# State-space scan and maxout FFN on one core: output pieces between the seam's y products, earlier output-weight decoding, later masks and exponents for the second chunk

## The chip, the cores and the metric

The kernel runs on one core of one Trainium2 chip. The metric is the device time of one execution in microseconds, and the time of a kernel is the median of its runs. The five engines of the core are called PE (matmul; PEld is its weight load), DVE, ACT, POOL and SP (which here only issues DMAs). Each engine takes its instructions strictly in the order in which the program gives them, and waits for others through semaphores.

## The reference

```python
# batch 4, heads 8, sequence 768, head_dim 32, d_state 16
log_a = np.log(np.clip(a, 1e-06, 1.0))
for c in range(nc):
    cum = np.cumsum(la, axis=-1)
    L = np.exp(cum[:, :, :, None] - cum[:, :, None, :]) * causal
    CB = np.einsum('bhin,bhjn->bhij', Cc, Bc)
    y_intra = np.einsum('bhij,bhjd->bhid', CB * L, xc)
    y_inter = np.einsum('bhin,bhnd->bhid', Cc, state) * np.exp(cum)[..., None]
    y[:, :, sl] = y_intra + y_inter
    state = decay_full * state + np.sum(Bx, axis=2)      # Bx: B x, decayed to the chunk's end
x = y.transpose(0, 2, 1, 3).reshape(3072, 256)           # the bridge
h = np.maximum(np.maximum(x @ w1, x @ w2), x @ w3)       # 256 -> 768
out = h @ w_out                                          # 768 -> 256
```

The weights come in 64-bit floats and are turned into 32-bit ones on the chip.

## The kernel before

The sequence is cut into six chunks of 128 tokens (all four batches and eight heads at once, so a chunk is 512 rows of the FFN). A chunk passes through the scan (transposes of B and C, scores s, masked decays L, state A, output y) and then through the FFN. The order of all instructions is written out by hand; nothing reorders them. While PE works on the FFN of one chunk, the pieces of the scan of the next one are put between its matmuls.

Chunk 0 and chunk 1 differ from the rest:

- **Chunk 0's FFN** is a loop over 18 groups (`for n in range(NF * 3)`, lines 1044 to 1105). A group is four matmuls of 128x512 in the trace (L648, two of the program's, each in two passes): one weight matrix, one 128-column slice. Groups 2j and 2j+1 use the weights that step j of the decoding has produced. Into these groups the scan of chunk 1 is placed: masks, exponents, transposes (`transposed(1)` at group 11), scores (group 12), state sums (group 14).
- **The decoding of a weight block** has six instructions on three engines: ACT L184 and L193, DVE L185 and L188, POOL L194 (`decode()`), and then DVE L197 (`sign()`), which writes the 32-bit block. There are nine blocks for w1 to w3 and three for `w_out`. A block is fetched by one DMA of 512 KB (L168).
- **The decays of chunk 1.** `decay_load` (L390) brings the sums of log a into the tile L by DMA; `decay_masks(1, 0)` and `decay_masks(1, 2)` (L405, POOL, two instructions each, one pair of batches each) write the causal mask; `part(1)` (L415, ACT, four instructions each, eight parts in all) takes the exponents; `scan_weight` (L560, DVE) multiplies the scores in. `pop` takes these and other postponed DVE steps from a list.
- **The seam** (lines 1106 to 1118) is the stretch between the last group of chunk 0 and the first group of the FFN of chunk 1. There PE forms y of chunk 1: `scan_old` (L572, 32 matmuls) and `scan_own` (L588, 64 matmuls in two calls of 32). Then ACT copies y out of PSUM (`scan_y`, L615), DVE forms sums of it (`scan_sums`, L623), and these feed the first group of chunk 1. B of chunk 2 is transposed in between (`transposed(2, False)`, L434).
- **Output pieces.** `down_next()` issues one of twelve pieces of chunk 0's output (L884, two matmuls of 128x256, four in the trace). Six pieces belong to one half u of the output. Within a half, pieces one and two read the first decoded block of `w_out`, three and four the second, five and six the third. Each half collects in one PSUM bank, of which there is one (`ffn_bank`). When a half is complete ACT copies it out (L889), and only then can the next half start.
- **The FFN of chunk 1** runs over nine groups k (`early` L713 to 727, `late` L729 to 745; seven matmul products L698 in place of eight). The tables X1, Y1, P1, D1, K1 say what goes where in these groups: X1 and Y1 name the output pieces ("D") and scan steps ahead of and behind `late`, P1 how many postponed steps are popped at three places, D1 which exponents (L415) of chunks 2 and 3 are taken, K1 the masks.

Sum banks, exponents and copies: in each group ACT first copies a sum out of PSUM (L723, in `early`), then takes D1's exponents, and then comes whatever X1 gives it.

Of the kernel before, what the change touches and what calls it, by code (L numbers as in the profile page):

```python
# [19 lines left out]
def kernel(  # L20
# [25 lines left out]
    NB, NH, S, D = x.shape  # L46
# [42 lines left out]
    def att_bank(shape, name):  # L89
        turn["att"] += 1  # L90
        if shared["att"] and turn["att"] % 5 == 0:
            return bank("sumA", 1, shape, name)
        return bank("att", 4, shape, name)
# [112 lines left out]
    def decode():  # L206

        first, second = decode_steps()
        first()
        unsigned.append(second)  # L210

    def sign():

        unsigned.pop(0)()
# [186 lines left out]
    def decay_masks(c, b0):  # L401

        b = slice(b0, b0 + 2)
        for rows, base in ((P, HP), (HP, 0)):
            nc.gpsimd.affine_select(  # L405
                out=Ls[c][0:rows, b], in_=Ls[c][0:rows, b],
                pattern=[[0, 2], [0, NH], [1, HP]], compare_op=ALU.is_ge, fill=MASKED,
                base=base, channel_multiplier=-1)
# [153 lines left out]
    def scan_old(c):  # L562


        st = blocks[c]
        st["y"] = ys = [[att_bank([P, NB, HP], "y") for _ in range(2)] for _ in range(KD)]
        for b in range(NB):
            for u, S in enumerate((states[c], middle[c])):
                for r in range(NP):
                    rows = slice(r * PN, (r + 1) * PN)  # L570
                    q = r % 2 * 2 * D
                    nc.tensor.matmul(  # L572
                        out=ys[r // 2][u][q:q + 2 * D, b],
                        lhsT=S[rows, b].rearrange("p g d -> p (g d)"),
                        rhs=st["Cd"][rows, b, u * HP:(u + 1) * HP],
                        start=(b == 0), stop=False, tile_position=(r * PN, q),
                        skip_group_check=True)

    def scan_own(c, bs=range(NB)):

        st = blocks[c]
        M = Ls[c]
        for b in bs:
            for h in range(NH):
                t, q = divmod(h, QH)
                for u in range(2):
                    rows = slice(u * HP, (u + 1) * HP)
                    nc.tensor.matmul(  # L588
                        out=st["y"][t][u][q * D:(q + 1) * D, b],
                        lhsT=st["x"][rows, b * NH + h], rhs=M[rows, b, h],  # L590
                        start=False, stop=True, tile_position=(u * HP, q * D),
                        skip_group_check=True)
# [111 lines left out]
    def pop(n):  # L704
        while n and later:
            later.pop(0)()
            n -= 1
# [154 lines left out]
    def add_downs(c):  # L862
        if c == 0:
            downs.extend((u, i, f) for u in range(2) for f in range(0, NF, 2) for i in range(2))
        elif c < NC - 2:
            downs.extend((c, u, which) for u, which in (
                (0, (1,)), (0, (6, 5)), (0, (7,)), (0, (2, 3, 4)), (1, (1, 6)), (1, (5, 7)),
                (1, (2, 3, 4))))
# [141 lines left out]
    def part(c, n=1):  # L1010
        for _ in range(n):
            if parts.get(c):
                decay_part(*parts[c].pop(0))
# [30 lines left out]
    for n in range(NF * 3):  # L1044
        j, g = divmod(n, 2)
        q, i = divmod(j, 3)
        f = 2 * q + g
        if n == 0:
            pair = [ffn_bank([P, BLK], "up") for _ in range(2)]
            group(pair[0], 0, 0, (0,))  # L1050
            first_own((2, 3))
            group(pair[1], 0, 1, (0,))
            for p, ff in zip(pair, range(2)):
                group(p, 0, ff, (1,))
        if j > 0:
            p = ffn_bank([P, BLK], "up")
            whole_group(p, i, f)
        else:
            p = pair[g]
        if i == 0 and g == 0:  # L1060
            m = ffn.tile([P, 4, HB], FP32, tag="m", name="m")
        pop({13: 2, 14: 1, 15: 2, 16: 1}.get(n, 0))
        mg = m[:, 2 * g:2 * g + 2].rearrange("p r t -> p (r t)")
        if i == 0:
            nc.scalar.copy(out=mg, in_=p)
        else:
            nc.vector.tensor_tensor(
                out=mg if i == 1 else h_of(0)[:, f], in0=mg, in1=p, op=ALU.max)
        if g == 0 and n <= 16:
            sign()  # L1070
            if n <= 14:
                decode()
        if n == 1:
            fj = from_last(R, a_sb, "fj", HP)
            decay_masks(1, 0)
        if n == 3:
            first_tokens()
            load(2, "B")
            fetch()
            load(2, "C")  # L1080
            fetch()
            decay_load(2, (0,))
            last_load(2)
            home(2, "x")
        if n == 6:
            decay_masks(1, 2)
        if n in (5, 7, 8, 9, 10, 11, 12, 13):
            part(1)
        if n == 11:
            transposed(1)  # L1090
            scan_bd(1)
            scan_c(1)
        if n == 12:
            scan_e(1)
            scan_cd(1)
            scores(1)
        if n == 14:
            later.extend(scan_state(1, att_bank))
        if n == 15:
            shared["att"] = False  # L1100
            places()
            weight_sums(0)
        if n == 17:
            decode()
            weight_sums(1)
    shared["ffn"] = False
    scan_old(1)
    scan_own(1, (0, 1))
    add_downs(0)
    down_next()  # L1110
    scan_own(1, (2, 3))
    sign()
# [8 lines left out]


    X1 = ["tc", "D", "DD", "s", "D", "AD", "D", "y", "DD"]
    Y1 = ["", "", "D", "", "", "D", "", "", ""]
    P1 = [(1, 0, 0), (1, 0, 0), (1, 0, 1), (1, 1, 1), (0, 0, 1), (1, 1, 2), (1, 0, 0), (1, 0, 1),
          (1, 1, 2)]
    D1 = [(0, 0), (0, 0), (2, 0), (2, 0), (2, 0), (2, 0), (0, 2), (0, 1), (0, 2)]
    K1 = {0: (0, 0), 1: (0, 2), 3: (1, 0), 5: (1, 2)}
    X2 = ["t", "s", "AD", "D", "D", "y", "D", "D", "D"]
# [7 lines left out]
    for c in range(1, NC):  # L1137
        n = c + 1
        xs, ys, ps_, ds, ks = (
            (X1, Y1, P1, D1, K1) if c == 1 else (X2, Y2, P2, D2, K2) if n < NC else  # L1140
            (X3, Y3, P3, D2, {}))
        for k in range(NW):
            if k == 0 and n == NC:
                pop(1)
            early(c, k)
            if c == 1 and k == 0:
                decode()
            if c == 1 and k == 1:
                sign()
            part(n, ds[k][0])  # L1150
            part(n + 1, ds[k][1])
            pop(ps_[k][0])
            if k == 0 and c > 1:
                if n < NC:
                    scan_bd(n)
                hidden_sums(c - 1, nc.gpsimd, (0 if c < NC - 1 else NQ - 1, NQ))
            if c >= NC - 2 and k in (3, 6):
                hidden_sums(c, nc.gpsimd, (k // 3 - 1, k // 3))
            x = xs[k]
            if n == NC:  # L1160
                last_next(k)
            elif x in ("D", "DD"):
                for _ in x:
                    down_next()
            elif x == "AD":
                later.extend(scan_state(n, att_bank))
                down_next()
            elif x == "tc":
                scan_tc(n, att_bank)
                down_next()  # L1170
            elif x == "t":
                transposed(n)
            elif x == "s":
                scores(n)
            elif x == "y":
                scan_old(n)
                scan_own(n)
                scan_y(n)
                scan_sums(n)
            pop(ps_[k][1])  # L1180
            maximum = late(c, k)
            if c == 1 and k + 2 < NW:
                weight_sums(k + 2)
            if c == 1 and k == NW - 2:
                output_weight_sums()
            if n < NC and k == 0:
                loads(c + 2)
            if n < NC and k == 0:
                scan_c(n)
            if n < NC and k == int(c == 1):  # L1190
                scan_e(n)
                later.append(lambda: scan_cd(n))
            flush()
            pop(ps_[k][2])
            later[:0] = maximum
            if ys[k] == "D":
                down_next()
                flush()
            if k in ks and n + ks[k][0] < NC:
                decay_masks(n + ks[k][0], ks[k][1])  # L1200
        if n == NC:
            pop(9)
        add_downs(c)
# [31 lines left out]
```

## Time and profile before

| | |
|---|---|
| median of 7 runs | 295.48 us (291.09 to 296.18) |
| the runs | 293.68, 291.09, 295.48, 296.03, 296.12, 296.18, 293.18 us |
| profiled execution, its own time | 293.68 us |
| its span in the profile | 292.0 us |
| mean granted TensorE clock | 0.994 |
| PE busy | 277.6 us (95%) |
| PEld / DVE / ACT / POOL busy | 77% / 71% / 38% / 42% |
| PE's share of the chain that ended last | 77% |

The profile is of one execution. Busy time is by engine; a wait is the idle time of an engine ahead of an instruction and is put down to what ended it. "issue" is a wait that no event in the profile explains. The granted clock is 1.00 where TensorE runs at full speed.

### The profile page before, as it was taken

How to read it: one execution, taken by the hardware profiler on the slowest of the kernel's cores; microseconds unless marked ns; L12 is line 12 of the kernel's file. 1: busy time of each engine (PE TensorE's matmuls, PEld its weight loads, DVE VectorE, ACT ScalarE, POOL GpSimd, SP SyncE). 2: the span in 40 equal slices, each digit the busy share in tenths (PEclk: the TensorE clock that was granted, in tenths of full speed). 3: DMA queues.
4: the chain of work that ended last, by engine and by line, in shares of the span. 5: the costliest groups of instructions: out<-in, count | busy, mean ns of one | idle time of the engine just before them, and what ended most of it. 6: DMA issues, size and time to landing. Idle time of an engine off the chain costs nothing.

```text
span 292.0 us, 7408 instructions
## 1 busy us (share of the span) xinstructions
PE 277.6 (95%) x3004; PEld 224.8 (77%) x3004; DVE 206.4 (71%) x414; ACT 112.2 (38%) x335; POOL 122.0 (42%) x143
## 2 busy tenths in 40 slices
PE   6899799979999999999999999999999999999995
PEld 4665345558788877888987888987888978989885
DVE  3586577955788757785867785867885876677682
ACT  2777399325354556233426233427212101011101
POOL 5173574593994874924003934004550403030300
PEclk9999999989999999999999999999999999999999
DMA  7969979979980008861006881001001001000103
GB/s 87 198 200 252 214 143 180 181 151 175 182 96 23 1 4 205 86 74 38 2 0 162 105 97 40 2 0 38 2 0 38 2 0 36 3 0 0 38 0 108
DMA packets 88957, 23.11 MB, mean 79 GB/s; under 512 B 80988, under 2 KB 84572, under 8 KB 88924
## 3 DMA queue, kind: packets, MB, share of 16 engines
q1 hardware_dynamic: 88476, 22.39, 42.5%
q8 instruction: 23, 0.38, 0.6%
q10 hardware_dynamic: 448, 0.26, 0.3%
q14 instruction: 10, 0.08, 0.1%
HBM read 19.40 MB, written 3.34 MB: 78 GB/s over the span
## 4 chain that ended last, share of the span: by engine, by line
PE 77%; DVE 11%; DMA 5%; issue 2%; ACT 1%; POOL 1%; SPq 0%; ACTq 0%; DVEq 0%; POOLq 0%
PE sumB L698 24%; PE sumA L698 18%; PE o L808 14%; PE up L648 7%; PE o L884 3%; PE y L588 3%; PE s L552 2%; DMA L<-cums 2%; PE y L572 2%; DMA rows_dram<-a_sb 2%; PE spread L335 1%; DVE v L725 1%; PE A L504 1%; DVE m L743 1%; DVE eu L724 1%
## 5 line engine op out<-in xcount | busy, mean ns | idle before, releaser
L698 PE MATMUL sumA<-yT,w 128*128 128x256 f32 x180 | 55.2, 389 | 0.9 <-DVE m L739 0.4
L783 POOL TENSOR_TENSOR hs<-h 128x256 f32<-128x256 f32 (+1 forms) x8 | 9.2, 1150 | 100.9 <-DVE h L743 100.9
L698 PE MATMUL sumB<-rb 128*128 128x256 f32 x180 | 46.2, 379 | 0.0
L723 ACT COPY eu<-sumA 128x256 f32<-128x256 f32 x45 | 16.8, 373 | 74.7 <-PE sumA L698 56.7
L415 ACT ACTIVATE L<-L,ncums 128x64 f32<-128x64 f32 x160 | 41.3, 339 | 2.4 <-POOL L L405 2.4
L698 PEld LDWEIGHTS sumB<-rb 128*128 128x128 f32 x180 | 34.2, 190 | 4.7
L698 PEld LDWEIGHTS sumA<-yT,w 128*128 128x128 f32 x180 | 31.0, 192 | 5.7 <-DVE m L739 0.8
L648 PE MATMUL up<-yT,w 128*128 128x512 f32 x64 | 29.1, 599 | 1.8 <-DVE w L197 1.8
L740 DVE TENSOR_TENSOR rb<-sumB,eu 128x512 f32<-128x512 f32 x30 | 20.7, 691 | 13.1 <-PE sumB L698 13.0
L724 DVE TENSOR_TENSOR eu<-sumA,eu 128x256 f32<-128x256 f32 x45 | 18.9, 421 | 14.9 <-ACT eu L723 14.4
L698 PE MATMUL sumB<-yT,rb 128*128 128x256 f32 x90 | 28.1, 393 | 1.0 <-DVE m L726 0.6
L698 PE MATMUL sumB<-rb,w 128*128 128x256 f32 x90 | 26.8, 379 | 0.4 <-issue 0.4
L194 POOL TENSOR_TENSOR w_u<-w_u,w_r 128x512 uint32<-128x512 uint32 x12 | 15.2, 1268 | 28.4 <-DVE w_u L188 20.6
L698 PE MATMUL sumA<-rb 128*128 128x256 f32 x90 | 26.8, 380 | 0.0
L405 POOL TENSOR_SCALAR_AFFINE_SELECT L<-L 128x1024 f32<-128x1024 f32 (+1 forms) x20 | 25.5, 1273 | 2.5 <-DMA L<-cums 1.8
L648 PEld LDWEIGHTS up<-yT,w 128*128 128x128 f32 x64 | 11.7, 190 | 15.8 <-issue 11.6
L725 DVE TENSOR_TENSOR v<-sumB,eu 128x256 f32<-128x256 f32 x45 | 19.1, 425 | 4.7
L698 PEld LDWEIGHTS sumB<-yT,rb 128*128 128x128 f32 x90 | 15.8, 189 | 7.3 <-DVE m L726 3.3
L698 PEld LDWEIGHTS sumB<-rb,w 128*128 128x128 f32 x90 | 17.1, 190 | 2.9 <-issue 0.6
L698 PEld LDWEIGHTS sumA<-rb 128*128 128x128 f32 x90 | 17.3, 192 | 2.5
L808 PE MATMUL o<-wo,h 128*128 128x128 f32 x120 | 17.6, 280 | 0.6 <-DVE ob L817 0.6
L808 PEld LDWEIGHTS o<-wo,h 128*128 128x128 f32 x120 | 15.9, 191 | 2.8 <-ACT eu L723 1.1
(141 smaller groups left out, 492.5 us busy)
## 6 DMA issues: line engine op xcount, KB each, us to landing
L<-cums SPq DMA_DIRECT2D x20, 256.0 KB, 5.4
rb<-in_moe_w_dram SPq DMA_DIRECT2D x9, 512.0 KB, 6.2
raw_x<-in_x_dram SPq DMA_DIRECT2D x6, 512.0 KB, 7.2
out_dram<-ob SPq DMA_DIRECT2D x11, 256.0 KB, 2.1
raw_B<-in_B_dram SPq DMA_DIRECT2D x6, 256.0 KB, 5.8
raw_C<-in_C_dram SPq DMA_DIRECT2D x6, 256.0 KB, 6.7
rb<-in_moe_w_out_dram SPq DMA_DIRECT2D x3, 512.0 KB, 6.1
E<-cums SPq DMA_DIRECT2D x40, 32.0 KB, 4.0
```

Of the source, the lines that this page charges most:

```text
L194: nc.gpsimd.tensor_tensor(out=u, in0=u, in1=r, op=ALU.add)
L405: nc.gpsimd.affine_select(out=Ls[c][0:rows, b], in_=Ls[c][0:rows, b], pattern=[[0, 2], [0, NH], [1, HP]], compare_op=ALU.is_ge, fill=MASKE ...
L415: nc.scalar.activation(L[:, b, h], L[:, b, h], AF.Exp, bias=ncum[c][:, b * NH + h:b * NH + h + 1], scale=1.0)
L588: nc.tensor.matmul(out=st["y"][t][u][q * D:(q + 1) * D, b], lhsT=st["x"][rows, b * NH + h], rhs=M[rows, b, h], start=False, stop=True, til ...
L648: nc.tensor.matmul(out=bank, lhsT=w_sb[i][:, k, f * P:(f + 1) * P], rhs=yT[0][:, k], start=(k == 0), stop=(k == KD - 1))
L698: nc.tensor.matmul(out=bank[:, half], lhsT=left(p, k), rhs=sides[c][p], start=(first and half == 0), stop=True, skip_group_check=True)
L723: nc.scalar.copy(out=eu[:, 0], in_=A[:, 0])
L724: nc.vector.tensor_tensor(out=eu[:, 1], in0=A[:, 1], in1=eu[:, 0], op=ALU.add)
L725: nc.vector.tensor_tensor(out=v, in0=B[:, 1], in1=eu[:, 1], op=ALU.add)
L740: nc.vector.tensor_tensor(out=t[:, 0:2], in0=B, in1=eu[:, 1:2].to_broadcast([P, 2, HB]), op=ALU.add)
L783: eng.tensor_tensor(out=s1, in0=a21, in1=a22, op=ALU.add)
L808: nc.tensor.matmul(out=o[:, PLACES[p]], lhsT=token_sums[c][p][:, f, u], rhs=wo_of(p)[:, f], start=(p == first and f == 0), stop=True, skip ...
```

## The change

- The second and third block of `w_out` begin their decoding at groups 16 and 17 of chunk 0; before, they began at group 17 and in group 0 of chunk 1. The last block is finished (`sign()`) in group 0 of chunk 1 and no longer in group 1.
- The masks of chunk 1 move from groups 1 and 6 to groups 6 and 8. Its eight parts of exponents move from groups 5, 7, 8, 9, 10, 11, 12, 13 (one each) to 8, 9, 9, 10, 11, 12, 13, 14.
- At the seam, y is formed in three stretches (old, own of batches 0 and 1, own of batches 2 and 3) with an output piece between each two. One piece more than before is issued there.
- The pieces behind `late` in groups 2 and 5 of chunk 1 go away (Y1), so both pieces of "DD" in group 8 are real ones; before, the second found an empty list. The pops of groups 7 and 8 take one DVE step from one group to the other.

```diff
         if g == 0 and n <= 16:
             sign()
-            if n <= 14:
-                decode()
+            decode()
         if n == 1:
             fj = from_last(R, a_sb, "fj", HP)
-            decay_masks(1, 0)
...
-        if n == 6:
-            decay_masks(1, 2)
-        if n in (5, 7, 8, 9, 10, 11, 12, 13):
-            part(1)
+        if n in (6, 8):
+            decay_masks(1, n - 6)
+        part(1, {9: 2}.get(n, int(n in (8, 10, 11, 12, 13, 14))))
...
     shared["ffn"] = False
     scan_old(1)
+    add_downs(0)
+    down_next()
     scan_own(1, (0, 1))
-    add_downs(0)
     down_next()
     scan_own(1, (2, 3))
     sign()
...
-    Y1 = ["", "", "D", "", "", "D", "", "", ""]
-    P1 = [(1, 0, 0), (1, 0, 0), (1, 0, 1), (1, 1, 1), (0, 0, 1), (1, 1, 2), (1, 0, 0), (1, 0, 1),
-          (1, 1, 2)]
+    Y1 = 9 * [""]
+    P1 = [(1, 0, 0), (1, 0, 0), (1, 0, 1), (1, 1, 1), (0, 0, 1), (1, 1, 2), (1, 0, 0), (1, 0, 2),
+          (1, 0, 2)]
...
             early(c, k)
             if c == 1 and k == 0:
-                decode()
-            if c == 1 and k == 1:
                 sign()
```

## The prediction

> **What bounds the kernel now.** I read the page first, then PE's instructions in order of time with the idle time ahead of each, then what released PE, then the clock by stretches of 3.41 us, and last the queues of ACT, POOL and DVE around each stop. PE works 277.6 of 292.0 us, so an edit counts only where it opens or closes a stop of PE or changes its clock. In the range that the change touches (26 to 110 us), these are PE's stops:
>
> ```profile
> PE 277.6 (95%) x3004; PEld 224.8 (77%) x3004; DVE 206.4 (71%) x414; ACT 112.2 (38%) x335; POOL 122.0 (42%) x143
> q8 instruction: 23, 0.38, 0.6%
> ...
> 32.86 7.13 PE L648 MATMUL up<-yT,w 128*128 128x512 f32 x16 [1.63 <-DVE w L197]
> 46.36 1.21 PE L552 MATMUL s<-CT,BT 32*64 32x128 f32 x64
> 59.15 1.13 PE L884 MATMUL o<-wo,h 128*128 128x256 f32 x4
> 60.21 0.57 PE L588 MATMUL y<-L,raw_x 64*32 64x64 f32 x35
> 62.38 0.45 PE L588 MATMUL y<-L,raw_x 64*32 64x64 f32 x29 [1.61 <-issue]
> 75.14 0.70 PE L698 MATMUL sumA<-yT,w 128*128 128x256 f32 x2 [0.44 <-DVE m L739]
> 104.82 0.59 PE L698 MATMUL sumB<-rb,w 128*128 128x256 f32 x2 [0.38 <-issue]
> ```
>
> See that the scores (46.36) have no wait in brackets today, and that two stops are "issue". Those two lie 1,024 PE records apart (weight loads and matmuls counted); the page's 23 instruction packets for 2 x 3004 records are 261 records each. So both stops are ends of a block of 256 instructions, and the next block was not there. In the trace, the packet ahead of the first stop ran from 59.58 to 60.85, and PE went on 1.53 us after its end; ahead of the second 102.39 to 103.35, and 1.47 us.
>
> The clock, in stretches of 3.41 us (columns: stretch, its length, busy time of PE, PEld, DVE, ACT, POOL, then the granted clock):
>
> ```profile
> 29.17:32.58 3.41, 2.07 (x5) 0.57 (x3) 1.16 (x2) 1.06 (x4) 2.84 (x3) 1.00 1.05 217
> 32.58:36.00 3.42, 3.14 (x8) 1.47 (x9) 2.28 (x5) 1.12 (x3) 1.27 (x1) 1.00 1.21 235
> 59.89:63.30 3.41, 1.42 (x67) 0.84 (x66) 0.93 (x1) 0.52 (x2) 3.33 (x5) 1.00 0.59 103
> 63.30:66.72 3.42, 3.42 (x11) 2.88 (x12) 2.68 (x4) 1.27 (x4) 2.26 (x4) 0.50 0.99 139
> ```
>
> A stretch with PE idle for 1.99 us was followed by 3.42 us at half clock, which costs 1.71. One with 1.34 idle was not.
>
> **The change part by part.**
>
> *Masks later: the stop at 32.86 goes.* POOL and ACT before:
>
> ```profile
> 28.50 2.36 POOL L405 TENSOR_SCALAR_AFFINE_SELECT L<-L 128x1024 f32<-128x1024 f32 x2 [1.80 <-DMA L<-cums]
> 30.83 1.25 POOL L194 TENSOR_TENSOR w_u<-w_u,w_r 128x512 uint32<-128x512 uint32 x1
> 37.11 1.27 POOL L194 TENSOR_TENSOR w_u<-w_u,w_r 128x512 uint32<-128x512 uint32 x1 [2.10 <-DVE w_u L188]
> 34.88 0.58 ACT L1065 COPY m<-up 128x512 f32<-128x512 f32 x1 [2.93 <-PE up L648]
> 39.20 2.00 ACT L415 ACTIVATE L<-L,ncums 128x64 f32<-128x64 f32 x8
> 44.80 1.27 ACT L449 ACTIVATE CT<-trC,parity 128x512 f32<-128x512 f32 x2
> 78.90 0.59 ACT L889 COPY ob<-o 128x512 f32<-128x512 f32 x1 [0.26 <-PE o L884]
> ```
>
> POOL stands at the mask until the DMA lands, and the decoding's add waits behind it. Without the mask the add starts when DVE's shift ends (27.79 + 0.43, plus 0.14 as in other rows: 28.36) and ends at 29.6. DVE reaches the sign at about 30.2 (behind the maximum of group 4 at 29.56) and ends it at 30.9. PE is due at 31.24. **-1.63**, with 0.3 to spare.
>
> *The same move puts a wait ahead of the scores.* All of group 6 comes 1.63 earlier. ACT's copy: 33.25. The two decoding steps behind it end at 35.0, DVE's two at 35.35, POOL's add runs 35.5 to 36.75. Only then come the masks in POOL's queue: 2.36 to 2.69 a pair (the second pair's row is 2.69), so 39.1 to 39.45. ACT has nothing to do from 36.8 on and then has, ahead of the copies that the scores need: twelve exponents (2.00 for eight, 1.06 for four, so 3.0), two decoding steps (1.15), eight exponents (1.97; the second pair of masks is ready at 43.1), BT (0.49) and CT (1.27). That ends between 46.95 and 47.3. PE is due at the scores at 46.36 - 1.63 = 44.73. It waits 2.2 to 2.6; if a pair of masks takes 3.08, as at 83.95, 3.0. **+2.3**. Before, six parts of exponents stood ahead of BT and were covered, because the first began at 30.89. The multiplications with the scores (L560) stay covered: the last part ends on ACT near 53, its DVE step is due at 54.
>
> *The seam.* PE comes 0.67 later to it. A piece costs 1.06 there (59.15 to 60.21); one more stands ahead of the block's end. PE came from the first old matmul (57.27) to the stop in 3.3; now 4.3, and the block ends eight records of y earlier. Its end is thus reached at 62.25. The block was entered, 256 records before its end, at 57.90 and the next one was there 4.48 later. Entered at 58.57 it comes at 63.05 if the queues are as full: the stop shrinks by 1.0. At the second stop it took 2.9 (101.92 to 104.82): then the stop goes, 1.6. If the fetch comes only when the DMAs around it are done, 0.5. **-1.0.** The piece itself is not extra work: twelve before, twelve after. The second "issue" stop: the block there ends two 128x256 matmuls later (0.86) for two of y (0.05), more than its 0.38: **-0.38**.
>
> The Trainium skill speaks against a gain here: "Runtime: NRT & Kernel Launch", section "Instruction fetch mechanics", says that blocks of 256 instructions are fetched while the current one runs, at a cost mostly hidden. The blocks agree with the count above; "mostly hidden" does not hold for stretches of small matmuls (1.61 and 0.38). By the page both terms were 0.
>
> *Decoding sooner.* ACT, DVE and POOL do the same steps earlier; no DMA is issued at another place in SP's queue. The third block's data landed at 59.66 in the trace, so ACT's steps end at 60.9, and y's copies (queued behind them) are due at 63.4. That cover is 2.5; a later landing would hold up y, its sums and the first group. POOL's add (1.25) goes ahead of the second group's weight sums, which end near 65.5 and are read at 69.5. Cost 0. The sign (1.39 at 73.37) leaves group 1, where it made PE wait: **-0.44**. In group 0 it stands where two decoding steps (0.88) stood, before an idle 0.85: 0.
>
> *The half's end in group 2.* The sixth and seventh piece now stand side by side, and the seventh needs the bank that ACT's L889 empties. ACT's queue in that group is: copy, eight exponents, L889. From the group's first matmul (75.14) the exponents end 3.50 later, L889 4.08 later; PE is through the sixth piece at 2.69. Before, `late` stood between (PE went on at 80.00, L889 was over at 79.49). **+1.4.** The pops of groups 7 and 8 put one DVE step of 0.42 ahead of a sum or behind it: -0.34 (a wait of PE there) to +0.42; the step has idle DVE time of 0.4 to 1.0 beside it, so I take 0.
>
> *The clock.* The seam keeps about 1.0 idle, less than the 1.34 that left the clock alone: **-1.71**. The wait at the scores is 2.3: by where the stretches happen to lie, one of them holds 1.99 or more of it in half of the positions and over 1.34 in nine of ten. Nearer the row with the drop: **+1.71**, ends 0 and 1.71. In group 2 the wait is 1.4, nearest the row without: 0, ends 0 and 1.71.
>
> "TensorE: Matmul & The Clock Gate", section "Part 1: The HAM clock gate", has a free-running window of 3.4 us (the trace's 3.42 agrees) and warns of idle gaps over about 3 us; by that neither wait drops the clock and the sum is 1.71 less. The row of 1.99 differs.
>
> **Sum:** -1.63 + 2.3 - 1.0 - 0.38 - 0.44 + 1.4 - 1.71 + 1.71 = +0.25. On the profiled execution: 293.68 + 0.25 = 293.9. It lies 1.8 below the median; that stays, so I forecast **295.7**, no change beyond 1% (a measurement of this kernel can tell about 1%, its runs spread by 1.7%). Its own range is 294 to 297.
>
> **Rivals.**
>
> 1. *The clock no longer drops.* Runs from 291.09 to 296.18 look like none, one and several drops. If neither ACT wait lowers it, each run is near the profiled sum without the last term, 292.2, and 291.6 with the block's wait gone. For it: only 1.99 idle is seen to do it. Against: 2.3 is more. 291.9, faster by 1.2%.
> 2. *ACT's queue sets the pace.* The masks take 3.08 as at 83.95, so the scores wait 3.0 (+0.7), and group 2's 1.4 lowers the clock as well (+1.71): 298.1, and 298.6 with the seam at its lower bound (+1.1%). It decides once idle of 1.4 in one stretch suffices, which lies between the two rows. Against: then the old stop of 1.63 lowered it in many runs too.
> 3. *The wait at the scores doesn't come*, ACT being faster than its rows: -2.3 - 1.71, 291.7. Nothing in the rows speaks for it.
>
> **Numbers.** Forecast 50%, first rival 22%, second 23%, third 5%. Rivals 1 and 3 make "faster by over 1%" 0.27; the second's upper half and a seam that gains nothing 0.23; the rest 0.50. The range goes to 291.2 and 299.0.
>
> **What would show it.** Right: no wait ahead of the matmuls near 31; a wait of 2 to 3 on CT ahead of the scores (L552) near 45; the "issue" stop in y under 1; a wait on L889 ahead of a piece near 76; half clock near 46 to 50 and none near 63. Wrong: no wait at the scores, an unchanged stop in y, or a new wait of more than 1 us elsewhere.

## The result and the profile after

The changed kernel takes 292.82 us (median of 27 runs, 292.04 to 298.03); the kernel before takes 294.13 us beside it (median of 64 runs). The ratio is 0.9958, interval 0.9941 to 0.9976: faster by 0.4%. That is 1.3 us, and 2.9 us under the forecast of 295.7.

Some executions of every kernel here have TensorE at half clock for 7 us or more in all (mean granted clock under 0.99) and are longer, the kernel before's beside e1 at 294.8 to 296.3 us and the changed kernel's of the first series at 297.4 to 298.0; "undisturbed" below means that these are left out, and the profile shown of the changed kernel is of an undisturbed execution (run e1, 292.37 us, span 290.6 us).

PE's stops in it, from its instructions in order of time (start, duration, engine, line, operation, tiles, count, and in brackets the idle time ahead and what ended it):

```profile
PE 276.5 (95%) x3004; PEld 223.0 (77%) x3004; DVE 210.1 (72%) x414; ACT 112.0 (39%) x335; POOL 123.3 (42%) x143
...
27.25 10.54 PE L648 MATMUL up<-yT,w 128*128 128x512 f32 x24
...
46.59 1.21 PE L552 MATMUL s<-CT,BT 32*64 32x128 f32 x64 [1.89 <-ACT CT L449]
61.49 0.86 PE L588 MATMUL y<-L,raw_x 64*32 64x64 f32 x64
65.37 0.67 PE L698 MATMUL sumA<-rb 128*128 128x256 f32 x2 [0.53 <-DVE rb L623]
77.17 1.13 PE L884 MATMUL o<-wo,h 128*128 128x256 f32 x4 [1.12 <-ACT ob L889]
```

The 24 matmuls from 27.25 run through: the stop of 1.63 is gone. The scores now have a bracket (1.89), y at 61.49 has none, the first group of chunk 1 has a new wait of 0.53 on DVE's sums (65.37), and the seventh piece waits 1.12 on L889. The clock in stretches of 3.41 us, around the scores and around the seam (columns as in the prediction):

```profile
42.21:45.62 3.41, 2.32 (x8) 0.77 (x5) 2.76 (x4) 3.41 (x12) 2.52 (x2) 1.00 0.93 226
45.62:49.03 3.41, 2.44 (x67) 1.64 (x68) 2.42 (x3) 3.41 (x10) 1.62 (x3) 1.00 1.68 140
59.28:62.69 3.41, 3.08 (x135) 2.03 (x133) 2.36 (x4) 1.66 (x4) 2.98 (x4) 1.00 0.19 43
62.69:66.10 3.41, 2.85 (x14) 2.16 (x15) 3.31 (x5) 1.33 (x5) 3.34 (x4) 1.00 1.21 151
```

Neither place is followed by half clock. The wait at the scores is split by the stretches' boundary at 45.62 (1.09 idle ahead of it, 0.97 behind). The same shows without a trace, in the mean clock of each run: 16 of the changed kernel's 18 undisturbed runs of the first series are at 0.999 or 1.000 (median 292.5; the record of clocks holds one run more than the 27 above). Of the kernel before's 20 undisturbed runs beside e1, 15 are near 0.993, which is one half-clock stretch (1.71 of 292 is 0.006), and only 5 near 1.000; the median of the 20 is 293.5. The five have a median of 292.7 and the fifteen of 293.9: where the kernel before keeps its clock it is about as fast as the changed one. By these runs the gain is that the drop of the clock has become rare, while the other terms nearly cancel; but the five may also have had a shorter stop in y, which their clocks don't show.

Where the time went between the two profiled executions, by the starts of three groups (the first L640, the first L572, the second chunk of scores at 82.68 and 81.25):

| stretch | before | after | difference | forecast for it |
|---|---|---|---|---|
| up to the first L640 | 19.10 | 18.79 | -0.31 | 0 (the change doesn't touch it) |
| to y of chunk 1 | 38.17 | 38.71 | +0.54 | -1.63 + 2.3 + 1.71 = +2.38 |
| y to the scores of chunk 2 | 25.41 | 23.75 | -1.66 | -1.0 - 0.44 + 1.4 - 1.71 = -1.75 |
| to the end | 209.32 | 209.35 | +0.03 | -0.38 |
| span | 292.0 | 290.6 | -1.40 | +0.25 |

### The profile page after: what moved, and what is told of

Same layout as the page of the kernel before. It is cut to its first block, busy times and chain, and to the rows that moved or that the text cites. A ratio compares the mean times of both kernels' runs of the same rounds, so it can differ in the third digit from the quotient of the medians.

```text
span 295.6 us, 7407 instructions
## 1 busy us (share of the span) xinstructions
PE 278.4 (94%) x3004; PEld 224.6 (76%) x3004; DVE 209.0 (71%) x414; ACT 112.0 (38%) x335; POOL 123.0 (42%) x143
## 4 chain that ended last, share of the span: by engine, by line
PE 61%; DVE 9%; issue 1%; ACT 1%; DVEq 0%; ACTq 0%
PE sumB L698 23%; PE sumA L698 16%; PE o L808 14%; PE y L588 2%; DVE rb L623 2%; PE s L552 2%; PE y L572 1%; DVE rb L740 1%; PE o L884 1%; DVE v L725 1%; DVE eu L724 1%; PE A L504 1%; DVE m L743 1%; DVE m L726 1%; DVE L L560 1%
## 5 line engine op out<-in xcount | busy, mean ns | idle before, releaser
L698 PE MATMUL sumB<-rb 128*128 128x256 f32 x180 | 47.0, 384 | 0.0
L698 PEld LDWEIGHTS sumB<-rb 128*128 128x128 f32 x180 | 34.8, 193 | 4.9
L648 PE MATMUL up<-yT,w 128*128 128x512 f32 x64 | 28.9, 599 | 0.4 <-DVE w L197 0.4
L405 POOL TENSOR_SCALAR_AFFINE_SELECT L<-L 128x1024 f32<-128x1024 f32 (+1 forms) x20 | 23.9, 1194 | 0.7
L648 PEld LDWEIGHTS up<-yT,w 128*128 128x128 f32 x64 | 11.7, 190 | 14.3 <-issue 11.7
```

The costliest lines, as they stand in the source:

```text
L405: nc.gpsimd.affine_select(out=Ls[c][0:rows, b], in_=Ls[c][0:rows, b], pattern=[[0, 2], [0, NH], [1, HP]], compare_op=ALU.is_ge, fill=MASKE ...
L648: nc.tensor.matmul(out=bank, lhsT=w_sb[i][:, k, f * P:(f + 1) * P], rhs=yT[0][:, k], start=(k == 0), stop=(k == KD - 1))
L698: nc.tensor.matmul(out=bank[:, half], lhsT=left(p, k), rhs=sides[c][p], start=(first and half == 0), stop=True, skip_group_check=True)
```

## The experiments

Undisturbed medians are compared with the kernel before's of the same comparison: 293.5 us beside e1 to e4, 293.4 beside e5 to e8, 294.5 beside e9 to e12, 292.8 beside e13 to e15. Each comparison ran on another chip, so differences are taken within one; where two are put side by side the shift between them is not known.

**e1: the changed kernel again.**

> The changed kernel once more, for a second profile of it. Theory A (each stop of PE is a term of its own; the clock stays full): wait of the scores on CT 1.9 us, issue stop in y 1.0, the seventh piece's wait on L889 1.1, granted clock 1.00 throughout, 292.0 to 292.9 us. Rival B (what the first profile of it showed at 65.85, the transposes' wait of 2.11 on y's copies behind the third output block's decoding, belongs to the change in every run): that wait is here again, a stretch of half clock follows it, and the time is 297 to 298.

Ratio 0.9995 (0.9946 to 1.0045), undisturbed 292.5, clock at 1.00 in 6 of 7. By this interval alone the gain could not be told from none; the 0.4% rests on the first series. Theory A held, but for the stop in y, which was 0 and not 1.0, and the new wait of 0.53. Its profile is the one above.

**e2: the later masks and exponents alone.** The kernel before with

```diff
         if n == 1:
             fj = from_last(R, a_sb, "fj", HP)
-            decay_masks(1, 0)
...
-        if n == 6:
-            decay_masks(1, 2)
-        if n in (5, 7, 8, 9, 10, 11, 12, 13):
-            part(1)
+        if n in (6, 8):
+            decay_masks(1, n - 6)
+        part(1, {9: 2}.get(n, int(n in (8, 10, 11, 12, 13, 14))))
```

> The kernel before with the later masks and exponents alone. Theory A: the wait of 1.63 on the sign ahead of the matmuls near 31 goes, the scores wait 1.9, the stop in y (1.61) and the half clock after it stay: +0.3, between 293.4 and 294.5, no difference. Rival B (the masks are what gains, the seam nothing): 292.5, as the whole change. Rival C (the wait at the scores lowers the clock, as was forecast): half clock near 46 to 50, 295 to 296.

Undisturbed 293.15, ratio 1.0024 (0.9976 to 1.0072): no gain that can be told from none. From the first L640 to y it takes 38.70 us, against 38.17 before and 38.71 after. So the masks alone make that row of the table: 1.63 saved, 1.90 spent at the scores. The seam is unchanged, its stop in y was 1.49, and yet 7 of 8 undisturbed runs were at full clock: the stretch there held 1.57 idle instead of 1.99. By theory A's terms a full clock there makes the time 1.4 shorter than before, and it is only 0.35. In this profile the way from y to the scores of chunk 2 is indeed 1.74 shorter (23.67 us), but the part behind them is 1.0 longer (210.3 us against 209.3; the second "issue" stop is 0.67 instead of 0.38, and a wait of 0.38 on L726 is new at 107.85).

```profile
62.72 0.45 PE L588 MATMUL y<-L,raw_x 64*32 64x64 f32 x29 [1.49 <-issue]
...
59.83:63.25 3.42, 1.85 (x68) 1.20 (x67) 0.85 (x1) 0.12 (x1) 3.34 (x5) 1.00 0.43 75
63.25:66.66 3.41, 3.11 (x16) 2.62 (x17) 2.83 (x6) 2.32 (x7) 2.56 (x4) 1.00 1.43 186
```

**e3: the changed kernel with the old masks and exponents** (e2's edit undone).

> The changed kernel with masks and exponents where they were before (seam pieces, sooner decoding and the tables stay). Theory A: the wait of 1.63 near 31 is back, the scores don't wait, the stop in y is 1.0 or less with no half clock after it: 0.3 less than the whole change, about 292. Rival B (the masks are what gains): 293.5 to 294.5, as before. If the clock still drops at the seam, 1.7 more than theory A.

Undisturbed 291.8, 1.7 below the kernel before; all 8 undisturbed runs at 1.000; ratio 0.9974 (0.9939 to 1.0008). Stop in y 0.83, wait on L889 1.12, stop near 31 back at 1.20. The forecast for these edits alone was -1.0 - 0.38 - 0.44 + 1.4 - 1.71 = -2.13. So, by the undisturbed medians, the seam's part brings the gain, and the masks' part takes some of it back (e1's 292.5 is 0.7 above e3); e3's interval just reaches 1.

**e4: the changed kernel with the third output block's decoding behind the transposes of chunk 2.**

```diff
         if n == 17:
-            decode()
             weight_sums(1)
...
     transposed(2, False)
+    decode()
     scan_bd(2)
```

> The changed kernel with the third output block's decoding issued behind y's copies and sums (ACT, DVE, POOL) in place of group 17; its sign stays in group 0 of chunk 1. Theory A: y's copies no longer stand behind a DMA; the wait of the transposes on y's copies is 0.4, the piece that reads the third block (group 1) waits for nothing; 292.3, like the changed kernel at its best, and no run near 297.8. Rival D (the late landing is not what holds the seam up): runs near 297.8 come as often as with the changed kernel.

Undisturbed 291.9, ratio 0.9981 (0.9947 to 1.0014); stop in y 1.2. No run came near 297.8, as theory A has it (the two longest took 296.5 and 296.7); two are too few to settle rival D. The waits on CT and L889 are as in e1, but e1's wait of 0.53 on DVE's sums is gone. The rows of e1 (the first two) and of e4 point to the reason:

```profile
62.76 1.59 POOL L194 TENSOR_TENSOR w_u<-w_u,w_r 128x512 uint32<-128x512 uint32 x1 [0.43 <-ACT yT L615]
63.14 1.49 DVE L623 TENSOR_TENSOR rb<-yT 128x256 f32<-128x256 f32 x1
```

```profile
64.49 0.42 DVE L623 TENSOR_TENSOR rb<-yT 128x256 f32<-128x256 f32 x1 [1.18 <-ACT yT L615]
```

In e1 the third block's add runs on POOL beside the first of DVE's sums, which takes 1.49; in e4 that add comes at 67.22, and the same sum takes 0.42.

In the first profiled execution of the changed kernel (297.40 us) the third block's decoding stood on ACT until its block landed, ahead of the copies of y:

```profile
64.32 0.66 ACT L184 ACTIVATE w_u<-rb 128x512 f32<-128x512 f32 x1 [5.44 <-DMA rb<-in_moe_w_out_dram]
...
65.44 1.18 ACT L615 COPY yT<-y 128x256 f32<-128x256 f32 x4
```

That is the cover of 2.5 us which the prediction named, gone: the block landed at 64.2 instead of 59.7. In e1 it holds (L184 at 59.58), and the move changes nothing in the time that the intervals can tell.

**e5, e6 and e12: the wait at the scores made longer.** The changed kernel with one part, two parts, or half a part of exponents moved ahead of BT and CT:

```diff
-        part(1, {9: 2}.get(n, int(n in (8, 10, 11, 12, 13, 14))))
# e5
+        part(1, {9: 2, 11: 2}.get(n, int(n in (8, 10, 13, 14))))
# e6
+        part(1, {9: 2, 11: 3}.get(n, int(n in (8, 10, 14))))
# e12 (decay_part gets an argument: which of its two batches)
+        part(1, {9: 2}.get(n, int(n in (8, 10, 11, 13, 14))))
+        if n == 11:
+            decay_part(1, *parts[1][0][1:], which=(0,))
+        if n == 12:
+            decay_part(1, *parts[1].pop(0)[1:], which=(1,))
```

> The changed kernel with one part of exponents (four instructions, 1.05 us on ACT) moved from group 12 to group 11, ahead of the copies BT and CT. PE then waits about 1.0 longer at the scores: 1.9 + 1.0 = 2.9. Theory (the clock halves after a stretch of 3.41 us in which PE was idle about 2.0 or more; the changed kernel's 1.9 stays below it): a wait of 2.9 falls with 2.0 or more into one stretch in two of three positions, so about two thirds of the runs show half clock for 3.4 us after the scores (+1.7) and the undisturbed runs lie 1.0 to 2.7 above the changed kernel's 292.4: median near 294.5, with two groups of runs. Rival (a wait on ACT never lowers the clock, only the stop at the block's end does): 293.4, one group, clock 1.00 throughout.

> The changed kernel with two parts of exponents (2.1 us on ACT) moved from groups 12 and 13 to group 11: the wait at the scores becomes about 3.9. Theory: whatever the position, a stretch of 3.41 us holds 1.95 or more of it, so nearly every run shows half clock behind the scores: 292.4 + 2.0 + 1.7 = 296.1, one group. Rival (waits on ACT do not lower the clock): 294.4, clock 1.00.

> The changed kernel with half a part of exponents (two instructions, 0.53 us on ACT) moved from group 12 to ahead of BT and CT: the wait at the scores becomes 2.4, which is what the prediction had for the changed kernel itself (2.3). Theory (the clock halves after a stretch with about 1.95 or more idle; stretches are 3.41 long and lie anywhere): with 2.4 the boundary misses in 1.5 of 3.41 positions, so about half of the runs (5 in 10) show 0.994, where 1.9 gives one in ten and 2.9 gave six in ten; times 292.9 without and 293.5 to 294.6 with. Rival (the clock depends on the single wait crossing a fixed length between 1.9 and 2.9, wherever the stretches lie): all runs alike, either all 1.000 or all 0.994.

| | wait at the scores | undisturbed runs with a half-clock stretch | undisturbed median | ratio |
|---|---|---|---|---|
| changed kernel (first series) | 1.89 | 2 of 18 | 292.5 | 0.9958 |
| e12 | 2.39 | 1 of 8 | 293.4 | 0.9952 (0.9921 to 0.9983) |
| e5 | 2.86 | 6 of 10 | 294.2 | 1.0043 (1.0011 to 1.0074) |
| e6 | 3.81 | 10 of 10 | 294.6 | 1.0056 (1.0024 to 1.0088) |

The kernel before lay at 293.4 beside e5 and e6 and at 294.5 beside e12, so the medians of the rows don't compare directly; the counts of runs do. The stretch that held the wait and the next one, in e5, then e6:

```profile
45.46:48.87 3.41, 1.44 (x65) 1.26 (x66) 1.98 (x2) 3.41 (x8) 1.28 (x2) 1.00 1.69 139
48.87:52.28 3.41, 3.41 (x5) 1.35 (x4) 2.33 (x5) 0.79 (x3) 1.26 (x1) 0.50 1.18 206
```

```profile
44.65:48.06 3.41, 0.12 (x8) 0.12 (x16) 1.56 (x1) 3.41 (x11) 1.65 (x2) 1.00 1.32 242
48.06:51.48 3.42, 3.42 (x66) 2.30 (x67) 2.29 (x5) 1.95 (x4) 1.27 (x1) 0.50 1.56 121
```

In e12's profile the stretch at the scores held 1.77 idle, and the next stayed at 1.00. So a wait on ACT does halve the clock behind it, and the rival of e5 and e6 falls: it depends on how much of the wait falls into one stretch (e5's two groups of runs speak against e12's rival, one fixed length, unless the wait itself varies from run to run). That none of the long waits escapes and six in ten of the middling do fits stretches that lie anywhere; the 1 in 8 of e12 was to be 5 in 10 by the same reckoning and misses it, so the share at 2.4 is not settled. The price was off as well. In e5's profile the way from the first L640 to y grew by 2.63 us, which is 0.97 of wait and 1.66 of clock; but the medians of e5's runs with and without the stretch (294.50 and 293.52) lie only 1.0 apart, and e6 lies 1.5 below its forecast. Part is given back later: in e6's profile 0.51 between y and the scores of chunk 2 (23.25 us against e1's 23.75; e1's wait of 0.53 on DVE's sums isn't there) and 0.4 behind them, in e5's 0.1 and 0.1. The rest these profiles don't show.

**e7: the seventh piece back behind `late` in group 2.**

```diff
-    X1 = ["tc", "D", "DD", "s", "D", "AD", "D", "y", "DD"]
-    Y1 = 9 * [""]
+    X1 = ["tc", "D", "D", "s", "D", "AD", "D", "y", "DD"]
+    Y1 = ["", "", "D"] + 6 * [""]
```

> The changed kernel with the seventh output piece put back behind late in group 2 of the second chunk's FFN. Theory (the 1.1 us at that piece is ACT's queue, and closing it costs nothing elsewhere): the wait on L889 is gone, the time is 1.1 lower than the changed kernel's 292.4, so 291.3; sums near 75 to 80 wait at most 0.5. Rival (DVE, whose maxima and sums set the pace of that group, gives the wait back at the next sum): a wait of 0.7 to 1.1 on DVE ahead of a sum L698 near 77 to 80 and 292.2 to 292.4.

As the theory said: undisturbed 290.95 against the changed kernel's 292.5, no wait on L889, and no bracket at PE's matmuls between 65 and 106 us (a piece at 64.71 waits 0.76 on the sign of an output block). The ratio is 0.9952 (0.9899 to 1.0004). From y to the scores of chunk 2: 22.68 us, 1.07 less than the changed kernel's 23.75.

**e8: the masks two groups earlier than in the change.**

```diff
-        if n in (6, 8):
-            decay_masks(1, n - 6)
-        part(1, {9: 2}.get(n, int(n in (8, 10, 11, 12, 13, 14))))
+        if n in (4, 6):
+            decay_masks(1, n - 4)
+        part(1, {12: 2}.get(n, int(n in (6, 7, 8, 9, 13, 14))))
```

> The changed kernel with the masks of the second chunk at groups 4 and 6 (two later than in the kernel before for the first pair, at the same place for the second) and its exponents at 6, 7, 8, 9, 12, 12, 13, 14. Theory (masks and exponents ahead of CT in ACT's and POOL's queues are all that holds up the scores): the wait of 1.9 at the scores goes, the old stop near 31 does not come back; the decoding's add of group 6 starts 0.5 later behind the first pair of masks, so a wait of 0 to 0.7 on the sign L197 near 38; together 1.2 to 1.9 below the changed kernel: 290.5 to 291.2. Rival (the scores have another wait right behind, on PSUM banks or on the last group's maximum): 0.7 or more stays ahead of the scores and the time is 291.7 or more.

The wait at the scores went (no bracket), and the time did not move: undisturbed 292.47, ratio 0.9980 (0.9945 to 1.0016). The sum failed at the signs:

```profile
32.37 2.69 POOL L405 TENSOR_SCALAR_AFFINE_SELECT L<-L 128x1024 f32<-128x1024 f32 x2
...
32.45 1.60 DVE L197 SCALAR_TENSOR_TENSOR w<-rb,w_u 128x512 uint32<-128x512 uint32 x1 [0.87 <-POOL w_u L194]
33.98 1.36 DVE L185 TENSOR_SCALAR w_u<-w_u 128x512 f32<-128x512 f32 x1
...
39.00 3.67 PE L648 MATMUL up<-yT,w 128*128 128x512 f32 x8 [1.20 <-DVE w L197]
```

While POOL writes the mask, DVE's L197 and L185 take 1.60 and 1.36, where each takes 0.69 and 0.42 alone. The decoding of group 4 is late by that, the next add starts at 35.95, and PE waits 1.20 at the sign near 38. Two waits of 0.27 and 0.28 inside the state sums (L504, 50.31 and 50.86) take most of the rest: from the first L640 to y it takes 38.54 us, against e1's 38.71. A stop of 0.89 in y (62.31) comes on top.

**e9, e11 and e13: pieces without sooner decoding, sooner decoding without pieces, both.** The kernel before with

```diff
# e9 and e13
     scan_old(1)
+    add_downs(0)
+    down_next()
     scan_own(1, (0, 1))
-    add_downs(0)
     down_next()
     scan_own(1, (2, 3))
...
-    X1 = ["tc", "D", "DD", "s", "D", "AD", "D", "y", "DD"]
+    X1 = ["tc", "D", "D", "s", "D", "AD", "D", "y", "DD"]
# e11 and e13
             sign()
-            if n <= 14:
-                decode()
+            decode()
...
             if c == 1 and k == 0:
-                decode()
-            if c == 1 and k == 1:
                 sign()
```

> The kernel before with the seam alone changed: y in three stretches with an output piece between each two, and the seventh piece left behind late in group 2. Masks, exponents and decoding stay as before, so the stop of 1.63 near 31 and the waits on the signs stay too. Theory (the seam is the change's gain: the stop at the block's end shrinks from 1.6 to 0 to 1.0, the idle time of the stretch falls under 1.9 and the half clock of 3.4 us behind it goes): nearly every run at granted clock 1.000 where the kernel before has 0.994, and 291.0 to 291.5, 2 to 2.5 below the kernel before's usual 293.6. Rival (the seam was not what lowered the clock; the later masks or the sooner decoding did): clock 0.994 in most runs and 292.6 or more.

> The kernel before with the sooner decoding of the second and third output block alone. Theory (the sign leaves group 1, where it made PE wait 0.44 on DVE; nothing else changes, the stop in y and the half clock behind it stay): 0.3 to 0.5 below the kernel before, clock 0.994 in most runs, stop of 1.4 to 1.6 in y. Rival (the third block's two steps on ACT stand ahead of y's copies and wait for that block's data): a wait of 0.5 or more on the y copies L615 ahead of trB near 63 and a time equal to the kernel before's or above.

> The kernel before with the third stretch and piece at the seam (seventh piece kept behind late) and the sooner decoding, masks and exponents as before. The pieces alone brought a wait of 2.34 on the sign of the third output block in group 1, the decoding alone nothing. Theory (the two need each other: the extra piece makes the fifth piece due one group earlier, and only the sooner decoding has its block ready): no wait on wo longer than 1.0, half clock near 63 in none of the undisturbed runs, 290.8 to 291.4. Rival (the gain of the third run with the old masks came from elsewhere, the new pops): 293 or more, or a wait of 1.5 or more on wo.

| | undisturbed | kernel before beside it | difference | ratio |
|---|---|---|---|---|
| e9, pieces | 294.6 | 294.5 | +0.1 | 0.9962 (0.9923 to 1.0002) |
| e11, decoding | 293.4 | 294.5 | -1.1 | 0.9981 (0.9943 to 1.0018) |
| e13, both | 291.1 | 292.8 | -1.7 | 0.9952 (0.9916 to 0.9989) |

By the ratios the two edits simply add up (0.9962 times 0.9981 is 0.994, e13 has 0.995), so the times don't show that they need each other. That is read from e9's profile:

```profile
72.50 1.38 DVE L197 SCALAR_TENSOR_TENSOR wo<-rb,w_u 128x512 uint32<-128x512 uint32 x1
73.93 1.13 PE L884 MATMUL o<-wo,h 128*128 128x256 f32 x4 [2.34 <-DVE wo L197]
...
72.01:75.42 3.41, 1.49 (x7) 1.34 (x8) 1.83 (x3) 0.00 (x0) 3.34 (x5) 1.00 1.49 158
75.42:78.83 3.41, 3.41 (x18) 3.00 (x17) 2.10 (x5) 1.53 (x7) 3.26 (x5) 1.00 1.01 227
```

With one more piece at the seam the fifth piece, the first that reads the third block, is due one group sooner, and with the old decoding its sign is just being written. As much as the seam can save is lost there. e11's gain can't be told from none by its interval: the wait of 0.44 in group 1 is gone, but its stop in y was 2.33, and 5 of its 6 undisturbed runs have the half clock. Of the three only e13 has an interval below 1, and 10 of its 11 undisturbed runs are at full clock. Its profile is of the eleventh, where the mask near 31 waited longer for its DMA (2.64 before L648, 2.33 idle in one stretch) and the half clock came there; its wait on the third block's sign was 1.24, over the 1.0 expected.

**e14: the first pair of masks one group later, nothing else.** The kernel before with

```diff
             fj = from_last(R, a_sb, "fj", HP)
-            decay_masks(1, 0)
...
-        if n == 6:
-            decay_masks(1, 2)
+        if n in (2, 6):
+            decay_masks(1, {2: 0, 6: 2}[n])
```

> The kernel before with one edit: the first pair of masks one group later, at group 2, behind the decoding's add. Theory (the stop of 1.63 near 31 is the add standing behind the mask, and 1 group is enough to end it): that stop gone, 0 to 0.5 on a sign near 34, no wait at the scores, the stop in y and mostly the half clock behind it as before: 1.1 to 1.6 below the kernel before's undisturbed 293.6, so 292.0 to 292.5. Rival (what is saved there is lost again at the block's end in y, which comes when it comes): the stop in y grows by 1.0 or more and the time stays at 293 or more.

The stop near 31 is gone and the scores don't wait, as the theory said, but the time is the kernel before's: undisturbed 292.8 against 292.8, ratio 1.0023 (0.9986 to 1.0061). Most of what was saved was lost again neither at the signs (0.19 and 0.24) nor in y, but at the state sums (the first row is of the kernel before, the others of e14):

```profile
43.53 0.47 SPq L134 DMA_DIRECT2D raw_x<-in_x_dram  x1
...
44.17 0.47 SPq L134 DMA_DIRECT2D raw_x<-in_x_dram  x1
51.28 0.85 PE L504 MATMUL A<-raw_x,Bd 64*32 64x64 f32 x64 [1.64 <-DVE m L1067]
DMA to landing us min/median/max: 7.0/7.0/7.0
```

The bracket names L1067, but that is not what held A: in the kernel before A began at 51.13, ahead of the start of that L1067 (52.13). Its input raw_x was issued at 44.17 and landed 7.0 later, at 51.2; in the kernel before it was issued at 43.53 and landed 6.9 later, at 50.4. So PE was there 1.5 sooner than before (49.64 against 51.13), and x 0.7 later. Neither theory had that wait. That raw_x is the cause is read from the times; no run with an earlier load was made.

**e10 and e15: a version from these readings.** e3 with e14's masks and e7's seventh piece:

```diff
# against the changed kernel
-        if n in (6, 8):
-            decay_masks(1, n - 6)
-        part(1, {9: 2}.get(n, int(n in (8, 10, 11, 12, 13, 14))))
+        if n in (2, 6):
+            decay_masks(1, {2: 0, 6: 2}[n])
+        if n in (5, 7, 8, 9, 10, 11, 12, 13):
+            part(1)
...
-    X1 = ["tc", "D", "DD", "s", "D", "AD", "D", "y", "DD"]
-    Y1 = 9 * [""]
+    X1 = ["tc", "D", "D", "s", "D", "AD", "D", "y", "DD"]
+    Y1 = ["", "", "D"] + 6 * [""]
```

> The changed kernel's seam, decoding and pops; the first pair of the second chunk's masks at group 2 (one later than before, behind the decoding's add and not ahead of it), all else of masks and exponents as before; the seventh piece behind late in group 2. Theory: the stop near 31 goes (1.2 to 1.6), since the add no longer stands behind the mask; the scores have no wait, since ACT has six parts done ahead of CT; no wait on L889 (1.1); the mask now stands ahead of group 4's add and costs 0 to 0.7 at a sign near 34; no half clock. Together 2 to 2.5 below the changed kernel's 292.4: 289.5 to 290.4. Rival (each removed wait is given back at a sign or at the first y copies): a wait of 1 or more on L197 near 34 to 38 and 291 or more.

> The combined version once more (the changed kernel's seam, decoding and pops, first masks at group 2, the rest of masks and exponents as before, seventh piece behind late), for an undisturbed profile and more runs. Theory: undisturbed runs at 290.4 to 291.2, all at clock 1.000, PE's longest wait between 20 and 115 us at most 1.1 (the third output block's sign or the block's end in y). Rival: a wait of more than 1.1 that the first profile did not show, and undisturbed runs above 291.5.

Ratios 0.9865 (0.9821 to 0.9910) and 0.9917 (0.9874 to 0.9960). Undisturbed runs: 290.4 to 291.2 (3) and 289.3 to 292.4 (7, median 290.2), below the kernel before beside them (294.5 and 292.8) and below the changed kernel's 292.5 of another comparison. e10's three lie above its forecast of 289.5 to 290.4; of e15's seven, six are at full clock, four lie below the forecast of 290.4 to 291.2, and one, at 292.4, above it. Both profiles have half clock from 16 to 26 us, so whether a wait like e14's is left in the others is not seen; in these two no wait between 36 and 115 us was above 1.22 (the third block's sign).

## Why the prediction was wrong, by its own steps

- **The clock behind the scores, +1.71: this is the step that failed.** It measured 0. The prediction had a wait of 2.3 and one half-clock stretch as likely as not, and put the whole of it into the sum of the likeliest case. The wait was 1.89, and 2 of 18 runs show a half-clock stretch (at what place, no trace says), which at 1.71 each is 0.2. It is the size of the idle time that decides: 1.92 in one stretch left the clock alone (e9), 1.98 did not (e5). By these rows, with 1.89 in all, no position of the boundary could do it but by other idle time beside it. Without the term the sum is -1.46, and the spans differ by -1.40. That they agree so closely is partly luck: -0.31 came ahead of anything that the change touches, the -0.38 did not come, and terms of the seam that were off cancel (below). This is the first rival, given 22%; its 291.9 is 0.9 below the median.
- **The offset to the median, "that stays", +1.8: wrong.** It was worked out from seven runs, of which four lay at 295.48 to 296.18. Beside e1, 15 of the kernel before's 35 runs lie at 294.8 to 296.3, so seven runs can well have their median among them. Over 64 runs the median is 294.13, 0.45 above the profiled execution, and not 1.8. The 1.35 between them and the 1.71 of the clock are the miss of 2.9.
- **The wait at the scores, +2.3: right in place and cause, 1.89 in size.** The masks began at 36.16 and 40.97, each pair 2.69; ACT came to CT at 45.30 and ended at 46.54, a little before the 46.95 worked out. Counted from the first L640 that is 27.75 instead of 27.85, while PE was ready for the scores at 25.91 instead of 25.63: most of the 0.4 is PE's own lateness.
- **The stop near 31, -1.63: right**, the sign now being written in time. e14 shows what the step left out: by itself that saving is worth nothing, because raw_x, which was 0.7 us ahead of its use in the kernel before, is next (and came 0.7 later there). In the changed kernel the wait at the scores covers that.
- **The seam's stop, -1.0 with ends 0.5 and 1.6: right in kind, and its size varies by execution.** What was left in y was 0.98 in the first profile, 0 in e1, 0.83 in e3, 1.2 in e4. By the prediction's own figures (the end reached at 62.25, the block there at 63.05) it would have shrunk by 0.8, not 1.0. The traces show with what the spread goes: all ten profiles with the stop have it ahead of the same record of PE, and PE goes on 1.28 to 1.53 after the end of an instruction packet that starts 1.56 to 2.67 after the record 256 places earlier; in the seven profiles without the stop it starts 0.69 to 1.38 after it. That e1 has no stop at all is thus luck; what delays the packet is not shown.
- **The clock at the seam, -1.71: right that the drop goes, too large in what it is worth.** Between the same matmuls, from B's transposes (63.21 before, 62.72 in e1) to the third output piece (68.41, 67.17), e1 takes 4.45 us instead of 5.20. That is 0.75, or 1.28 with e1's new wait of 0.53 taken off. The stop in y, which went by 1.61 in place of 1.0, makes up for it in the table. Nearly all undisturbed runs of e1, e3, e4, e7 and e8 are at full clock, where most of the kernel before's are not. The margin is thin: the kernel before held 1.99 there, just above the 1.98 of e5, and in e2 an unchanged seam with 1.49 of stop mostly escaped.
- **The sooner decoding "cost 0", the sign -0.44: the coupling was missed.** The wait of 0.44 is gone, but the step's larger worth is in the 2.34 of e9, which the extra piece cost without it (1.24 are left in e13, none in e1). Nor was its cost 0: the third block's add on POOL made DVE's sums of y late, by 0.53 in e1 and 0.34 in e3, and by nothing in e4, where the add comes later. That the piece is "not extra work: twelve before, twelve after" is true, and says nothing on when its weights are ready.
- **The seventh piece, +1.4: right, 1.12**, and e7 gets 1.07 of it back.
- **The second "issue" stop, -0.38: it is gone from e1's profile, and nothing is gained.** The part behind the scores of chunk 2 takes 209.35 us instead of 209.32; the bracket left there is 0.38 on L726 at 107.09, where the kernel before had 0.34 on L739 at 109.77, so what took the gain back the brackets don't show.

## What to carry to other kernels

A term that is all or nothing, such as a halved clock, and that comes in about half of the cases belongs into the chances and not in full into the sum; here a wait 0.4 shorter than worked out was enough to end it, because the known row (1.99) lay that close. When a stall is removed, look for the next input in line and its landing time, DMAs first: in e14 a wait of 1.64 for raw_x, as far as the times show, took back the whole gain. And when work is moved forward, ask of each piece behind it whether its operands are ready one place sooner: e9's piece, moved up by one, stood 2.34 us before a block that was not yet written.

## What the runs showed of the hardware that was not expected

**The clock's threshold.** Stretches between 30 and 80 us, PE idle in each and the clock of the next: 1.57 (e2), 1.77 (e12) and 1.92 (e9) are followed by full clock; 1.98 (e5), 1.99 (the kernel before), 2.26 (the first profile of the changed kernel), 2.33 (e11 and e13) and 3.29 (e6) by half. The Trainium skill, "TensorE: Matmul & The Clock Gate", section "Part 1: The HAM clock gate", asks for an idle window of some 3.4 us for the drop; in these runs 58% of one was enough, so the measurement decides. Nor is PE's idle time the whole measure. In e15's profile, where PE's work is the first chunk's small matmuls, 1.78 idle was followed by half clock, and that for three stretches:

```profile
12.72:16.13 3.41, 1.63 (x47) 1.14 (x40) 3.38 (x8) 3.41 (x7) 2.38 (x2) 1.00 1.13 297
16.13:19.55 3.42, 3.42 (x35) 2.27 (x30) 1.37 (x3) 0.10 (x1) 1.81 (x2) 0.50 0.59 218
```

**POOL's masks stretch DVE's steps.** L197 took 1.09 to 1.61 us (34 times in the 17 profiles) and L185 1.36 (28 times) beside a mask, against 0.68 to 0.69 (90 times) and 0.40 to 0.43 (149 times) with POOL idle (e8 above; in the kernel before L197 at 38.92 took 1.10 and L185 at 39.95 took 1.36 beside the mask at 38.33). The Trainium skill, "SBUF — State Buffer", section "Who interferes with whom", says that a DVE operation with two inputs from SBUF contends with a GpSimd operation that reads SBUF, and that one in a mode that uses two ports contends with GpSimd, where whoever issues second is blocked for the whole instruction of the other. The rows fit: 0.94 more for L185 is most of one mask instruction (2.69 for two). Whether L185 runs in such a mode no row here shows.
